# Linear attention and an MoE product: the feature map as a line and a minimum, rest rows on alternate partitions

## Chip, cores and metric

The kernel runs on one core of a Trainium2 chip. The metric is device time in microseconds (us), the median over runs; a run is one execution. The span of a profile is about 2 us shorter than the time of its run.

## The reference

Eight batches, eight heads, 576 rows of 64 numbers; attention with a feature map in place of the softmax, then two dense products with a gelu between them.

```python
def phi(x):
    return np.where(x > 0, x, np.exp(x) - 1.0) + 1.0
q_p, k_p = phi(q), phi(k)
kv = np.einsum('bhsd,bhse->bhde', k_p, v)
z = np.sum(k_p, axis=2)
num = np.einsum('bhsd,bhde->bhse', q_p, kv)
den = np.einsum('bhsd,bhd->bhs', q_p, z)[..., None] + 1e-06
x = (num / den)            # to [4608 tokens, 512]
h = x @ w_in               # 512 x 2048
g = 0.5 * h * (1.0 + np.tanh(c * (h + 0.044715 * h * h * h)))
out = g @ w_out            # 2048 x 512
```

576 rows are 4 x 128 (the main rows of a tile) and 64 more, the rest rows. A tile of rest rows holds the 64 of one even and one odd batch, 128 partitions in all.

## The kernel before

The schedule is written by hand: each engine runs its instructions in the order of the program. The parts that the argument touches are the first loads and the startup of batch 0.

```python
def load_rest_half(src, t, m, s, eng):
    eng.dma_start(
        out=t[REST * s : REST * (s + 1)],          # REST = 64: batch s of the pair
        in_=src[2 * m + s, :, MAIN:S, :].rearrange("h p d -> p h d"))
# ...
load_rest_half(k, ld["kr", 0], 0, 0, nc.sync)      # first half of k_r: batch 0
load_rest_half(v, ld["vr", 0], 0, 0, nc.sync)
ld["v", 0] = load_main(v, 0, "v_x", nc.sync, parts=2)
w_st = [load_w_in(0), load_w_in(1, None, slice(0, 256))]
ld["k", 1] = load_main(k, 1, "k_x", nc.sync)
load_rest_half(k, ld["kr", 0], 0, 1, nc.sync)      # second half of k_r: batch 1
load_w_in(1, w_st[1], slice(256, 512))
# ...
def phi_into(xp, x, e, hs):
    nc.vector.tensor_scalar(e[:, hs], e[:, hs], 1.0, None, op0=ALU.min)
    # ... for each chunk c:
        nc.vector.scalar_tensor_tensor(
            xp[:, c, hs, :], xv[:, c, hs, :], 0.0, ev[:, c, hs, :], op0=ALU.max, op1=ALU.add)
# ... startup of batch 0 ...
for n, e in (("k", ke), ("q", qe)):
    for s in halves:
        nc.scalar.activation(e[:, s], ld[n, 0][:, s], AF.Exp)
exp_rest_half("kr", kre, 0)                        # partitions 0 to 63 only
keep_warm(36)                                      # 72 small matmuls
# ... phi of k and q ...
for i in range(2):
    transpose_q(i, nc.scalar.copy)
keep_warm(5)
phi_rest_half("kr", kre, 0)
cast_v(0, nc.scalar.copy, halves[0])
cast_vr(0, (0,))
for i in range(2, NP):
    transpose_q(i, nc.scalar.copy)
# ... four kv groups, nab (the attention of one chunk), transposes, then the dense products
```

The names in the profile: `kr_e` is the exp of the rest rows of k, `kr_p` their phi, `t_ps` transposes, `qt` the transposed phi of q, `kv_ps` the groups of phi(k)^T v, `n_ps` a nab, `h_ps` and `o_ps` the two dense products, `w_ps` matmuls without use for the result, the warm-up, that are to keep the clock up.

Of the kernel before, what the change touches and what calls it, by code (L numbers as in the profile page):

```python
# [8 lines left out]
FP32 = mybir.dt.float32  # L9
BF16 = mybir.dt.bfloat16  # L10
# [5 lines left out]
def kernel(  # L16
# [8 lines left out]
):  # L25



    nc = tc.nc
# [45 lines left out]
    def load_rest_half(src, t, m, s, eng):  # L75
        eng.dma_start(
            out=t[REST * s : REST * (s + 1)],
            in_=src[2 * m + s, :, MAIN:S, :].rearrange("h p d -> p h d"),
        )
# [34 lines left out]
    for n in ("kr", "vr", "qr"):  # L114
        ld[n, 0] = prest.tile([P, H, D], FP32, name=n[0] + "_r")
    load_rest_half(k, ld["kr", 0], 0, 0, nc.sync)
# [11 lines left out]
    make_identity(nc, ident)  # L128
    vps = [const.tile([P, H, C, E], BF16, name=f"vp{i}") for i in range(2)]
# [5 lines left out]
    for i in range(2):  # L135
        nc.gpsimd.memset(vps[i][:, :, :, D:E], 1.0)
        for s in range(2):
            nc.gpsimd.memset(vrs[i][s], 0.0)
            nc.gpsimd.memset(vrs[i][s][REST * s : REST * (s + 1), :, D:E], 1.0)
        nc.gpsimd.memset(kvbds[i], 0.0)  # L140
# [22 lines left out]

    def exp_main(name, b):
        e = pe.tile([P, H, C * D], BF16, name=name + "_e")
        nc.scalar.activation(e, ld[name, b], AF.Exp)  # L166
        return e

    def phi_into(xp, x, e, hs):

        nc.vector.tensor_scalar(e[:, hs], e[:, hs], 1.0, None, op0=ALU.min)  # L171
        xv = x.rearrange("p h (c d) -> p c h d", d=D)
        ev = e.rearrange("p h (c d) -> p c h d", d=D)
        for c in range(xp.shape[1]):
            nc.vector.scalar_tensor_tensor(  # L175
                xp[:, c, hs, :], xv[:, c, hs, :], 0.0, ev[:, c, hs, :],
                op0=ALU.max, op1=ALU.add,
            )

    def phi_of(x, e, name):  # L180
        xp = pphi.tile([P, x.shape[2] // D, H, D], BF16, name=name)
        phi_into(xp, x, e, slice(0, H))
        return xp

    def phi_rest(name, m):
        x = ld[name, m]
        e = pe.tile([P, H, D], BF16, name=f"{name}_e{m % 2 if name == 'qr' else ''}")
        nc.scalar.activation(e, x, AF.Exp)
        return lambda: phi.__setitem__((name, m), phi_of(x, e, name + "_p"))

    def exp_rest_half(name, e, s):
        r = slice(REST * s, REST * (s + 1))
        nc.scalar.activation(e[r], ld[name, 0][r], AF.Exp)

    def phi_rest_half(name, e, s):
        r = slice(REST * s, REST * (s + 1))
        nc.vector.tensor_scalar(e[r], e[r], 1.0, None, op0=ALU.min)
        nc.vector.scalar_tensor_tensor(
            phi[name, 0][r, 0], ld[name, 0][r], 0.0, e[r], op0=ALU.max, op1=ALU.add
        )  # L200
# [7 lines left out]
    def cast_vr(m, halves=(0, 1)):  # L208
        for s in halves:
            r = slice(REST * s, REST * (s + 1))  # L210
            nc.vector.tensor_copy(out=vrs[m % 2][s][r, :, 0:D], in_=ld["vr", m][r])
# [103 lines left out]
    ke = pe.tile([P, H, C * D], BF16, name="k_e")  # L315
    qe = pe.tile([P, H, C * D], BF16, name="q_e")
    kre = pe.tile([P, H, D], BF16, name="kr_e")
# [4 lines left out]
    nc.gpsimd.memset(phi["kr", 0][REST:P], 0.0)  # L322
# [16 lines left out]
    for n, e in (("k", ke), ("q", qe)):  # L339
        for s in halves:  # L340
            nc.scalar.activation(e[:, s], ld[n, 0][:, s], AF.Exp)  # L341
    exp_rest_half("kr", kre, 0)
    keep_warm(36)
    for n, xp, e in (("k", kp, ke), ("q", qp, qe)):
        for s in halves:
            phi_into(xp, ld[n, 0], e, s)
# [3 lines left out]
    phi_rest_half("kr", kre, 0)  # L350
    cast_v(0, nc.scalar.copy, halves[0])
    cast_vr(0, (0,))
    for i in range(2, NP):
        transpose_q(i, nc.scalar.copy)
    keep_warm(2)
    for h in range(2):
        if h == 1:
            cast_v(0, nc.vector.tensor_copy, slice(4, 6))
            cast_v(0, nc.scalar.copy, slice(6, 8))
        kv_ps = ps_a.tile([P, 2, 512], FP32, name="kv_ps", tag="a")  # L360
        for i in range(2):
            kv_mm(0, 2 * h + i, kv_ps, i)
        kv_evac(0, kv_ps[:, 0:1], h, nc.scalar.copy)
# [32 lines left out]
    kre1 = pe.tile([P, H, D], BF16, name="kr_e")  # L396
    exp_rest_half("kr", kre1, 1)
# [14 lines left out]
    phi_rest_half("kr", kre1, 1)  # L412
# [109 lines left out]
    def plan_second():  # L522
# [4 lines left out]
        def exps():  # L527
            box["q"] = pe.tile([P, H, C * D], BF16, name="q_e")
            for s in halves:
                nc.scalar.activation(box["q"][:, s], ld["q", b][:, s], AF.Exp)  # L530
            gelu_table()

        def phis():
            phi["q", b] = pphi.tile([P, C, H, D], BF16, name="q_p")
            for s in halves:
                phi_into(phi["q", b], ld["q", b], box["q"], s)
# [166 lines left out]
    def second_half(j):  # L703
# [38 lines left out]
        3, (2, 1, 7), (2, 1, 15), None, (1, 2, 0), (1, 2, 1), None, (2, 1, 12)  # L742
    )
    plan_attention(3, 1, 2, (5, 6, 7, 8), (12, 13, 14, 15))
# [49 lines left out]
```

## Time and profile before

| | before |
|---|---|
| time | 296.47 us (296.12 to 297.66, 3 runs) |
| span of the profile | 293.8 us |
| TensorE busy | 286.3 us, 97% |
| first dense product starts | 20.67 us |
| from there to the end | 273.1 us |
| first exp of k_r | 11.11 us |
| load queue (q1) busy | 50.1% of the span, 147 us |

The lines that bear the bound are in the prediction. Two more are from TensorE's timeline (start, duration, engine and line, operation, output and inputs, count, and in brackets the idle time before and what ended it).

```profile
13.90 0.40 PE L219 MATMUL kv_ps<-vp,k_p 128*128 128x130 bf16 x4
...
15.72 0.40 PE L219 MATMUL kv_ps<-vp,k_p 128*128 128x130 bf16 x4 [0.78 <-DVE vp L203]
```

### The profile page before, as it was taken

To read this page: it belongs to the slowest core of one execution; us is meant where nothing else is said; L and a number is where in the kernel's file an instruction comes from. 1 tells how busy PE (TensorE), PEld (TensorE's weight loads), DVE (VectorE), ACT (ScalarE), POOL (GpSimd) and SP (SyncE) were. 2 spreads that over 40 equal slices of the span, in tenths; PEclk is the share of its full clock that TensorE was granted, GB/s the bytes per second of all DMA engines. 3 is DMA by queue (packets, MB, busy share of 16 engines).
4 is the path that set the end of the run, shared out by engine and by line. 5 is a ranking of instruction groups with operands and counts; after the bars stand their busy time and mean duration, and the time that the engine had idled before them with its cause. 6 is when DMAs were issued, how large, how long until landed. Compare 5 with 4: busy or idle time off the path is not lost.

```text
span 293.8 us, 4318 instructions
## 1 busy us (share of the span) xinstructions
PE 286.3 (97%) x1698; PEld 149.0 (51%) x1698; DVE 132.1 (45%) x244; ACT 159.6 (54%) x222; POOL 37.1 (13%) x56
## 2 busy tenths in 40 slices
PE   8979999999999999999999999999999999999995
PEld 6755456644565544544454445444554444444443
DVE  2969495328689488336524592346241000000002
ACT  4759843579955763567355925682560076017400
POOL 8047548300002500000000000000000000000000
PEclk9999999999999999999999999999999999999999
DMA  7999999991499999629925797304241110021032
GB/s 241 361 382 405 394 386 368 322 383 53 102 332 268 186 279 321 178 58 281 306 73 74 242 296 144 68 6 125 89 56 36 71 71 2 0 95 47 2 71 73
DMA packets 64260, 53.24 MB, mean 181 GB/s; under 512 B 31728, under 2 KB 57584, under 8 KB 64240
## 3 DMA queue, kind: packets, MB, share of 16 engines
q1 hardware_dynamic: 60816, 41.82, 50.1%
q10 hardware_dynamic: 2464, 8.52, 7.5%
q0 software_dynamic: 960, 2.62, 3.8%
q8 instruction: 13, 0.21, 0.3%
q14 instruction: 7, 0.06, 0.0%
HBM read 36.70 MB, written 9.44 MB: 157 GB/s over the span
## 4 chain that ended last, share of the span: by engine, by line
PE 91%; DVE 3%; DMA 3%; ACT 1%; issue 1%; SPq 0%; DVEq 0%
PE h_ps L301 42%; PE o_ps L718 41%; PE n_ps L253 3%; DMA q_x<-in_q_dram 3%; PE kv_ps L219 2%; PE o_ps L687 1%; PE t_ps L276 1%; DVE kvbd L242 1%; DVE x L265 1%; PE kv_ps L226 1%; SPq L67 0%; DVE q_p L175 0%; ACT q_e L341 0%; PE t_ps L247 0%; DVE xt L383 0%
## 5 line engine op out<-in xcount | busy, mean ns | idle before, releaser
L718 PE MATMUL o_ps<-w_out_sb,g 128*128 128x512 bf16 x560 | 124.6, 379 | 0.0
L301 PE MATMUL h_ps<-xt,w_in_sb 128*128 128x512 bf16 (+1 forms) x548 | 119.5, 365 | 0.2
L675 ACT ACTIVATE g<-h_ps 128x512 bf16<-128x512 f32 x144 | 83.8, 598 | 48.1 <-PE h_ps L301 47.6
L718 PEld LDWEIGHTS <-g 128*128 128x128 bf16 x560 | 54.2, 98 | 62.6
L301 PEld LDWEIGHTS <-w_in_sb 128*128 128x128 bf16 x612 | 57.7, 98 | 54.7 <-issue 0.5
L733 ACT COPY o_sb<-o_ps 128x512 f32<-128x512 f32 x18 | 10.6, 586 | 56.5 <-PE o_ps L718 56.5
L731 DVE COPY o_sb<-o_ps 128x512 f32<-128x512 f32 x17 | 11.7, 688 | 62.4 <-PE o_ps L718 62.3
L265 DVE TENSOR_TENSOR x<-n_ps,r 128x512 bf16<-128x512 f32 x36 | 24.9, 691 | 1.2
L175 DVE SCALAR_TENSOR_TENSOR q_p<-q_x,q_e 128x512 bf16<-128x512 f32 (+1 forms) x40 | 24.1, 663 | 0.3
L175 DVE SCALAR_TENSOR_TENSOR k_p<-k_x,k_e 128x512 bf16<-128x512 f32 (+1 forms) x36 | 22.0, 674 | 0.3
L242 DVE CAST kvbd<-kv_ps 64x260 bf16<-64x260 f32 (+1 forms) x16 | 6.5, 409 | 28.0 <-PE kv_ps L226 27.9
L171 DVE TENSOR_SCALAR k_e<-k_e 128x2048 bf16<-128x2048 bf16 (+1 forms) x9 | 6.3, 705 | 27.6 <-ACT k_e L166 22.9
L263 DVE RECIPROCAL r<-n_ps 128x8 f32<-128x8 f32 x36 | 7.4, 206 | 24.6 <-PE n_ps L253 24.6
L301 PE MATMUL h_ps<-xt_rest,w_in_sb 128*128 128x512 bf16 x64 | 14.0, 379 | 0.0
L328 PE MATMUL w_ps<-warm 128*128 128x252 bf16 x94 | 12.7, 295 | 1.1 <-DVE warm L127 1.1
L253 PEld LDWEIGHTS <-qt 128*128 128x128 bf16 x128 | 9.7, 98 | 7.9 <-issue 1.1
L166 ACT ACTIVATE k_e<-k_x 128x2048 bf16<-128x2048 f32 x7 | 13.4, 1910 | 0.1
L253 PE MATMUL n_ps<-kvbd,qt 128*128 128x130 bf16 x128 | 12.7, 221 | 0.6 <-ACT kvbd L242 0.3
L219 PEld LDWEIGHTS <-k_p 128*128 128x128 bf16 x128 | 9.7, 96 | 6.8 <-issue 1.4
L219 PE MATMUL kv_ps<-vp,k_p 128*128 128x130 bf16 x128 | 12.2, 220 | 0.9 <-DVE vp L203 0.8
L145 ACT ACT_TABLE_LOAD x8 | 10.3, 1283 | 4.6 <-DVE o_sb L731 4.5
L166 ACT ACTIVATE q_e<-q_x 128x2048 bf16<-128x2048 f32 x6 | 11.4, 1894 | 0.0
(58 smaller groups left out, 144.6 us busy)
## 6 DMA issues: line engine op xcount, KB each, us to landing
out_dram<-o_sb ACTq DMA_DIRECT2D x16, 512.0 KB, 3.9
k_x<-in_k_dram SPq DMA_DIRECT2D x7, 1024.0 KB, 6.4
v_x<-in_v_dram SPq DMA_DIRECT2D x7, 1024.0 KB, 11.8
q_x<-in_q_dram SPq DMA_DIRECT2D x6, 1024.0 KB, 8.4
w_st<-in_moe_w_out_dram SPq DMA_DIRECT2D x4, 1024.0 KB, 10.8
w_st<-in_moe_w_in_dram SPq DMA_DIRECT2D x3, 1024.0 KB, 8.2
q_x<-in_q_dram SPq DMA_DIRECT2D x4, 512.0 KB, 9.3
k_x<-in_k_dram SPq DMA_DIRECT2D x2, 512.0 KB, 4.2
```

What stands on the lines that cost most here:

```text
L145: nc.scalar.preload_act_table_set("gelu_apprx_tanh_and_others")
L166: nc.scalar.activation(e, ld[name, b], AF.Exp)
L175: nc.vector.scalar_tensor_tensor(xp[:, c, hs, :], xv[:, c, hs, :], 0.0, ev[:, c, hs, :], op0=ALU.max, op1=ALU.add,)
L219: nc.tensor.matmul(dst, lhsT=kp[:, c, P * i : P * (i + 1)], rhs=vps[b % 2][:, 2 * i : 2 * i + 2, c, :], start=(c == 0), stop=False,)
L253: nc.tensor.matmul(n_ps[rows, i // 2, 2 * E * (i % 2) : 2 * E * (i % 2) + 2 * E], lhsT=qt_c[:, i, rows], rhs=kvbd[:, i, :], skip_group_che ...
L265: nc.vector.tensor_tensor(x, n_v[:, :, :, 0:D], r[:, :, :, None].to_broadcast([P, 2, 4, D]), op=ALU.mult,)
L301: nc.tensor.matmul(h_ps[:, tok], lhsT=w_in_sb[:, c, P * m : P * (m + 1)], rhs=xt[:, c, tok], start=(c == 0), stop=(c == KM - 1), skip_grou ...
L328: nc.tensor.matmul(w_ps[:, 0:252], lhsT=warm[:, 0:P], rhs=warm)
L675: nc.scalar.activation(gs[j][:, i, :], ps, AF.Gelu_apprx_tanh)
L718: nc.tensor.matmul(o_pss[t], lhsT=g[:, m, P * t : P * (t + 1)], rhs=w_out_sb[:, m, :], start=(m == 0), stop=(m == MM - 1),)
L731: nc.vector.tensor_copy(dst, o_ps)
L733: nc.scalar.copy(dst, o_ps)
```

## The change

Its intent is to relieve VectorE and to shorten the startup. Phi becomes min(exp(x), max(x + 1, 1)), a line and a minimum on a whole tile in place of one minimum and four fused adds. The rest rows of k and v go to even and odd partitions, so that each half load spreads over all of SBUF's partitions, with a mask that blanks the other batch's rows of v. The first tile of v is cast half by VectorE and half by ScalarE (before, three quarters by ScalarE), one copy of qt moves to VectorE, and batch 3 makes phi of q before phi of k. Cut to its core:

```diff
     def load_rest_half(src, t, m, s, eng):
+        rows = slice(REST * s, REST * (s + 1)) if src is q else slice(s, P, 2)
-            out=t[REST * s : REST * (s + 1)],
+            out=t[rows], in_=...
...
     for n in ("kr", "vr", "qr"):
         ld[n, 0] = prest.tile([P, H, D], FP32, name=n[0] + "_r")
+        if n != "qr":
+            nc.vector.memset(ld[n, 0], 0.0)
...
+    mask = const.tile([P, 2], FP32, name="mask")
+    nc.vector.tensor_reduce(mask, ident.rearrange("p (r s) -> p s r", s=2), axis=..., op=ALU.add)
...
+        nc.vector.tensor_scalar(xp..., by_chunk(x[:, hs]), 1.0, 1.0, op0=ALU.add, op1=ALU.max)
+        nc.vector.tensor_tensor(xp..., xp..., e..., op=ALU.min)
...
-    exp_rest_half("kr", kre, 0)
+    exp_into(kre, ld["kr", 0])
...
-    cast_v(0, nc.scalar.copy, halves[0])
+    phi_line(phi["kr", 0], ld["kr", 0])
+    phi_min(phi["kr", 0], kre)
...
     for h in range(2):
-        if h == 1:
-            cast_v(0, nc.vector.tensor_copy, slice(4, 6))
-            cast_v(0, nc.scalar.copy, slice(6, 8))
+        cast_v(0, nc.vector.tensor_copy, slice(4 * h, 4 * h + 2))
+        cast_v(0, nc.scalar.copy, slice(4 * h + 2, 4 * h + 4))
...
-        3, (2, 1, 7), (2, 1, 15), None, (1, 2, 0), (1, 2, 1), None, (2, 1, 12)
+        3, (2, 1, 7), (1, 2, 0), None, (1, 2, 1), (2, 1, 15), None, (2, 1, 12)
```

More of the change, by code (lines that the diff above doesn't have):

```diff
@@ L75, in load_rest_half @@
     def load_rest_half(src, t, m, s, eng):
+        rows = slice(REST * s, REST * (s + 1)) if src is q else slice(s, P, 2)
         eng.dma_start(
-            out=t[REST * s : REST * (s + 1)],
-            in_=src[2 * m + s, :, MAIN:S, :].rearrange("h p d -> p h d"),
+            out=t[rows], in_=src[2 * m + s, :, MAIN:S, :].rearrange("h p d -> p h d")
         )
@@ L128 @@
     make_identity(nc, ident)
+    mask = const.tile([P, 2], FP32, name="mask")
+    nc.vector.tensor_reduce(
+        mask, ident.rearrange("p (r s) -> p s r", s=2), axis=mybir.AxisListType.X, op=ALU.add
+    )
     vps = [const.tile([P, H, C, E], BF16, name=f"vp{i}") for i in range(2)]
@@ L137 @@
         for s in range(2):
-            nc.gpsimd.memset(vrs[i][s], 0.0)
-            nc.gpsimd.memset(vrs[i][s][REST * s : REST * (s + 1), :, D:E], 1.0)
+            nc.vector.tensor_copy(
+                out=vrs[i][s][:, :, D:E],
+                in_=mask[:, s : s + 1, None].to_broadcast([P, H, 1]),
+            )
         nc.gpsimd.memset(kvbds[i], 0.0)
@@ L162, with by_chunk, exp_into, phi_line @@
     phi = {}
+    def by_chunk(x):
+        return x.rearrange("p h (c d) -> p h c d", d=D)
+    def exp_into(e, x, hs=slice(0, H)):
+        nc.scalar.activation(
+            e[:, :, hs, :].rearrange("p c h d -> p h c d"), by_chunk(x[:, hs]), AF.Exp
+        )
     def exp_main(name, b):
-        e = pe.tile([P, H, C * D], BF16, name=name + "_e")
-        nc.scalar.activation(e, ld[name, b], AF.Exp)
-        return e
-    def phi_into(xp, x, e, hs):
-        nc.vector.tensor_scalar(e[:, hs], e[:, hs], 1.0, None, op0=ALU.min)
-        xv = x.rearrange("p h (c d) -> p c h d", d=D)
-        ev = e.rearrange("p h (c d) -> p c h d", d=D)
-        for c in range(xp.shape[1]):
-            nc.vector.scalar_tensor_tensor(
-                xp[:, c, hs, :], xv[:, c, hs, :], 0.0, ev[:, c, hs, :],
-                op0=ALU.max, op1=ALU.add,
-            )
+        e = pe.tile([P, C, H, D], BF16, name=name + "_e")
+        exp_into(e, ld[name, b])
+        return e
+    def phi_line(xp, x, hs=slice(0, H)):
+        nc.vector.tensor_scalar(
+            xp[:, :, hs, :].rearrange("p c h d -> p h c d"), by_chunk(x[:, hs]),
+            1.0, 1.0, op0=ALU.add, op1=ALU.max,
+        )
+    def phi_min(xp, e, hs=slice(0, H)):
+        nc.vector.tensor_tensor(
+            xp[:, :, hs, :], xp[:, :, hs, :], e[:, :, hs, :], op=ALU.min
+        )
     def phi_of(x, e, name):
         xp = pphi.tile([P, x.shape[2] // D, H, D], BF16, name=name)
-        phi_into(xp, x, e, slice(0, H))
+        phi_line(xp, x)
+        phi_min(xp, e)
         return xp
@@ L186, in phi_rest @@
         x = ld[name, m]
-        e = pe.tile([P, H, D], BF16, name=f"{name}_e{m % 2 if name == 'qr' else ''}")
-        nc.scalar.activation(e, x, AF.Exp)
+        e = pe.tile([P, 1, H, D], BF16, name=f"{name}_e{m % 2 if name == 'qr' else ''}")
+        exp_into(e, x)
         return lambda: phi.__setitem__((name, m), phi_of(x, e, name + "_p"))
-    def exp_rest_half(name, e, s):
-        r = slice(REST * s, REST * (s + 1))
-        nc.scalar.activation(e[r], ld[name, 0][r], AF.Exp)
-    def phi_rest_half(name, e, s):
-        r = slice(REST * s, REST * (s + 1))
-        nc.vector.tensor_scalar(e[r], e[r], 1.0, None, op0=ALU.min)
-        nc.vector.scalar_tensor_tensor(
-            phi[name, 0][r, 0], ld[name, 0][r], 0.0, e[r], op0=ALU.max, op1=ALU.add
-        )
     def cast_v(b, fn, s=slice(0, H)):
@@ L209, in cast_vr @@
         for s in halves:
-            r = slice(REST * s, REST * (s + 1))
-            nc.vector.tensor_copy(out=vrs[m % 2][s][r, :, 0:D], in_=ld["vr", m][r])
+            nc.vector.tensor_scalar(
+                vrs[m % 2][s][:, :, 0:D], ld["vr", m], mask[:, s : s + 1], None, op0=ALU.mult
+            )
     def kv_mm(b, i, kv_ps, at_i=None):
@@ L313, in first_mm_early @@
         first_mm(j, m, hs[j, m], slice(0, MAIN // 2))
-    ke = pe.tile([P, H, C * D], BF16, name="k_e")
-    qe = pe.tile([P, H, C * D], BF16, name="q_e")
-    kre = pe.tile([P, H, D], BF16, name="kr_e")
+    ke = pe.tile([P, C, H, D], BF16, name="k_e")
+    qe = pe.tile([P, C, H, D], BF16, name="q_e")
+    kre = pe.tile([P, 1, H, D], BF16, name="kr_e")
     kp = pphi.tile([P, C, H, D], BF16, name="k_p")
@@ L321 @@
     phi["kr", 0] = pphi.tile([P, 1, H, D], BF16, name="kr_p")
-    nc.gpsimd.memset(phi["kr", 0][REST:P], 0.0)
     qt = pt.tile([P, C, NP, P], BF16, name="qt")
@@ L340 @@
         for s in halves:
-            nc.scalar.activation(e[:, s], ld[n, 0][:, s], AF.Exp)
-    exp_rest_half("kr", kre, 0)
+            exp_into(e, ld[n, 0], s)
+    exp_into(kre, ld["kr", 0])
     keep_warm(36)
@@ L345 @@
         for s in halves:
-            phi_into(xp, ld[n, 0], e, s)
+            phi_line(xp, ld[n, 0], s)
+            phi_min(xp, e, s)
     for i in range(2):
@@ L349 @@
     keep_warm(5)
-    phi_rest_half("kr", kre, 0)
-    cast_v(0, nc.scalar.copy, halves[0])
+    phi_line(phi["kr", 0], ld["kr", 0])
+    phi_min(phi["kr", 0], kre)
     cast_vr(0, (0,))
     for i in range(2, NP):
-        transpose_q(i, nc.scalar.copy)
+        transpose_q(i, nc.scalar.copy if i == 2 else nc.vector.tensor_copy)
     keep_warm(2)
     for h in range(2):
-        if h == 1:
-            cast_v(0, nc.vector.tensor_copy, slice(4, 6))
-            cast_v(0, nc.scalar.copy, slice(6, 8))
+        cast_v(0, nc.vector.tensor_copy, slice(4 * h, 4 * h + 2))
+        cast_v(0, nc.scalar.copy, slice(4 * h + 2, 4 * h + 4))
+    for h in range(2):
         kv_ps = ps_a.tile([P, 2, 512], FP32, name="kv_ps", tag="a")
@@ L395 @@
     ke1 = exp_main("k", 1)
-    kre1 = pe.tile([P, H, D], BF16, name="kr_e")
-    exp_rest_half("kr", kre1, 1)
+    kre1 = pe.tile([P, 1, H, D], BF16, name="kr_e")
+    exp_into(kre1, ld["kr", 0])
     gelu_table()
@@ L411 @@
     phi["k", 1] = phi_of(ld["k", 1], ke1, "k_p")
-    phi_rest_half("kr", kre1, 1)
+    phi_line(phi["kr", 0], ld["kr", 0])
+    phi_min(phi["kr", 0], kre1)
     wo_st = [load_w_out(0)]
@@ L527, in exps @@
         def exps():
-            box["q"] = pe.tile([P, H, C * D], BF16, name="q_e")
+            box["q"] = pe.tile([P, C, H, D], BF16, name="q_e")
             for s in halves:
-                nc.scalar.activation(box["q"][:, s], ld["q", b][:, s], AF.Exp)
+                exp_into(box["q"], ld["q", b], s)
             gelu_table()
@@ L535, in phis @@
             for s in halves:
-                phi_into(phi["q", b], ld["q", b], box["q"], s)
+                phi_line(phi["q", b], ld["q", b], s)
+                phi_min(phi["q", b], box["q"], s)
         def cast_vs():
@@ L741 @@
     plan_prepare(
-        3, (2, 1, 7), (2, 1, 15), None, (1, 2, 0), (1, 2, 1), None, (2, 1, 12)
+        3, (2, 1, 7), (1, 2, 0), None, (1, 2, 1), (2, 1, 15), None, (2, 1, 12)
     )
-    plan_attention(3, 1, 2, (5, 6, 7, 8), (12, 13, 14, 15))
+    plan_attention(3, 1, 2, (7, 8, 9, 10), (12, 13, 14, 15))
     for b in range(4, B):
```

## The prediction

> **What bounds the kernel now.** I read the engine shares and the chain that ended last first, then the timeline of the first 24 us one engine at a time, then the DMA view of single stretches for landings.
>
> ```profile
> PE 286.3 (97%) x1698; PEld 149.0 (51%) x1698; DVE 132.1 (45%) x244; ACT 159.6 (54%) x222; POOL 37.1 (13%) x56
> ...
> PE 91%; DVE 3%; DMA 3%; ACT 1%; issue 1%; SPq 0%; DVEq 0%
> ```
>
> The reader is to see that TensorE bounds the whole, and that the 45% of VectorE, which most of the change relieves, hardly stands on the chain. From the first product at 20.67 us on, 512-column matmuls follow each other at 0.216 us and the gaps that I find (evacuations of kvbd near 47 and 77 us, the last xt copy near 54 and 85 us) sum to about 1.1 us of 273. So only the first 20.67 us can move the end by much. There:
>
> ```profile
> 10.14 1.06 ACT L341 ACTIVATE q_e<-q_x 128x1024 bf16<-128x1024 f32 x1 [0.95 <-DMA q_x<-in_q_dram]
> 11.11 0.61 ACT L193 ACTIVATE kr_e<-k_r 64x512 bf16<-64x512 f32 x1
> 11.63 1.04 ACT L337 COPY qt<-t_ps 128x512 bf16<-128x512 bf16 x2
> 12.57 1.05 ACT L203 CAST vp<-v_x 128x1024 bf16<-128x1024 f32 x1
> 13.52 1.06 ACT L337 COPY qt<-t_ps 128x512 bf16<-128x512 bf16 x2
> ...
> 20.65 1.91 ACT L166 ACTIVATE k_e<-k_x 128x2048 bf16<-128x2048 f32 x1
> 22.59 0.63 ACT L193 ACTIVATE kr_e<-k_r 64x512 bf16<-64x512 f32 x1
> ```
>
> ScalarE is a queue in order: the exp of the first rest rows (partitions 0 to 63) stands ahead of all copies of qt. The rest rows of the second batch have an exp of their own, 11 us later. TensorE in the same time:
>
> ```profile
> 10.42 1.22 PE L336 MATMUL t_ps<-ident,q_p 128*128 128x128 bf16 x8
> 11.48 1.24 PE L328 MATMUL w_ps<-warm 128*128 128x252 bf16 x10
> 12.55 1.08 PE L336 MATMUL t_ps<-ident,q_p 128*128 128x128 bf16 x8
> ...
> 17.45 0.51 PE L253 MATMUL n_ps<-kvbd,qt 128*128 128x130 bf16 x6 [0.34 <-ACT kvbd L242]
> ...
> 20.67 1.04 PE L301 MATMUL h_ps<-xt,w_in_sb 128*128 128x256 bf16 x8
> ```
>
> And when the two late loads land, from the DMA view of the stretch 11 to 12 us (last column: us from issue to landing):
>
> ```profile
> k_x<-in_k_dram SPq DMA_DIRECT2D x1, 1024.0 KB, 10.2
> k_r<-in_k_dram SPq DMA_DIRECT2D x1, 128.0 KB, 9.7
> ```
>
> This k_r is the second half of the rest rows, issued at 11.40 us: it lands at 11.40 + 9.7 = 21.1 us. The DMA engines are full here (the page has a 9 in every slice from 7 to 66 us), so it can't come much sooner.
>
> **What the Trainium skill says.** (1) "VectorE: DVE Perf Modes", the perf-mode tier table: 2048 fp32 elements through a one-source op from SBUF take 1227 ns, a two-source op 1224 ns in bf16 and 2293 ns with fp32. The trace agrees where it can: the cast of v (f32 to bf16, 2048 elements) took 1222 ns, four two-source ops on 512 f32 each 2.50 us. (2) The same page, "Zero memsets can be issued as uint32": a memset costs a cycle per element. The trace: 126 elements in 163 ns, so I estimate 512 at 0.56 us. (3) "TensorE: Matmul & The Clock Gate", Part 1: after an idle window of some 3.4 us the array runs at half rate until it has been busy for about as long. The trace shows the start of that: warm-up matmuls average 418 ns around 3 us and 271 ns from 5 us on. (4) "SBUF — State Buffer", Door 1: partitions 0 to 63 reach 8 of 16 DMA ports; every second partition reaches all. No trace here tests it yet; it would help 128 KB loads by tenths of a us.
>
> **The change part by part.**
>
> Feature map: a full tile before is one min (0.69 us) and four adds (2.50), 3.2 us; after, a line x+1, max 1 (1.22, as the cast of v) and a min in bf16 (1.22), 2.45 us. Over 13 full-size tiles that is about 10 us of VectorE work, nearly all beside a busy TensorE: worth nothing there. For q's second half at the start: it lands at 10.12, its exp ends at 11.21 as before, the line (half of 1.22 and a fixed part, 0.69) lies beside the exp, only the min (0.69) follows: q_p at 11.9 instead of 13.13 us, 1.2 us sooner.
>
> Memsets: two of 512 f32 now stand on VectorE before the one that the warm-up waits for: 2 x 0.56 = 1.1 us. The 72 warm-up matmuls, 1.05 to 10.42 us, end at 11.5, so the transposes start 1.1 us later. With the fixed pads behind them, the second pair of transposes starts at 11.5 + 0.44 + 1.07 = 13.0 us, against 12.55. Most of the 1.2 us is given back.
>
> v by both engines: one of the copies of qt moves to VectorE, and all casts of v now stand before the first evacuation, so the waits for v ahead of the third and fourth kv groups (0.78 and 0.16 us) go. Laid out from the row lengths (0.52 a copy, 0.62 a cast on ScalarE, 0.41 on VectorE), this would bring the last nab start from 17.45 to about 16.7 us: 0.8 us saved, if nothing else happened.
>
> The new wait: something else happens. Before, the exp covered partitions 0 to 63, which the first rest load alone fills. Now the rows of the two batches are interleaved, so the exp and the line take all 128 partitions, and both k_r loads are written ahead of that exp in the program. In the order of built instructions this exp waits for the first load's semaphore and for the second's: a count of 32 on the semaphore that q's second half (16) and then the second k_r load raise. The VectorE line waits for the same 32; and the second exp of k_r, at 22.59 us before, has lost its DMA wait. v_r is free of it, as its second load stands later in the program. So ScalarE stops at 11.2 and goes on at 21.1 us.
>
> From there: exp to 21.75, copies of qt to 22.3, 22.8, 23.3; the fourth transpose needs the PSUM buffer that the first copy frees, so TensorE stands idle from 13.3 to 22.35 us, far over the idle window: I take it at half rate at first. Transposes and their copy on VectorE to 23.4; v casts on VectorE to 24.0 and 24.5 (GpSimd's weight casts beside them stretch them; a similar op took 1.33 instead of 0.69 us at 22.59), on ScalarE to 23.95 and 24.6. Four kv groups at half rate (5 matmuls of 0.11, 0.54 each) from 24.05 to 26.2, drained 26.4; evacuations 0.29 and 0.27 with their gaps to 27.05. The last nab start is then 27.1 against 17.45: +9.6 us. The way to the first product was 3.2 us; the slower array adds an estimated 0.4. Sum: +10.0 us at the first product.
>
> Behind it TensorE's work is the same instruction for instruction, so the shift stays. Loads and weight casts, which don't wait for this, get about 10 us of slack.
>
> Batch 3's q first: kv moves from slot 5 to slot 7. VectorE has line, min, line, min, v cast, 5 x 1.22 = 6.1 us from 84.9, to 91.0 in the old clock; slot 7 begins at 89.38 + 8 x 0.216 = 91.1. No gain, and at most 0.2 us lost.
>
> Sum: 296.5 + 10.0 = 306.4 us, rounded.
>
> **The rivals.** (a) The wait costs nothing, because the second load comes early: then +0.8 us is won and the time is about 295.7. Against it: 21.1 us by the landing, and the second load sits behind 1 MB of k in a full queue. Rows spread over all ports would save tenths. (b) The startup gets shorter but weights or q of batch 1 become the bound: phi of batch 1's q ended at 41.54 with its transposes at 41.65, no margin, so the old feature map would have eaten such a gain; the new one frees it. Only matters with (a). (c) The array stays warm through the stop: then the last nab start comes 1.1 us sooner, the 0.4 falls away, and the shift is about 8.5, 305.0 us. (d) It stays at half rate into the dense products: the first 3.4 us of these would lose 1.7 us, about 308. For (c) speaks that no profile here shows an idle of 9 us; for (d), that TensorE is only partly busy from 22 to 30 us. I take the middle.
>
> **Range and chances.** From (c) with a landing half a us sooner, 304.4, to (d), 308.4. Faster than 290.5 isn't within reach of a 20 us startup that loses no work: 0.01. Within 2% needs a shift under 5.9 us, which only (a) gives: 0.05. Slower: 0.94.
>
> **What would show it.** ScalarE's k_r exp, 128 partitions, starts at about 21 us after some 10 us idle ended by DMA k_r. The first warm-up matmul starts at 2.1 to 2.2 us. The line and the min on 2048 elements read near 1.22 us each. The first product starts at 30 to 31 us, matmuls near 23 to 26 us at twice their length; from there to the end some 273 us as before. I am wrong if the k_r exp starts near 11 us; if the DMA view has the second k_r landing well before 20; or if time is lost or won after the first product.

## More of the kernel before

```profile
GB/s 241 361 382 405 394 386 368 322 383 53 102 332 268 186 279 321 178 58 281 306 73 74 242 296 144 68 6 125 89 56 36 71 71 2 0 95 47 2 71 73
...
q1 hardware_dynamic: 60816, 41.82, 50.1%
```

A group of four kv matmuls takes 0.40 us at full clock. One slice is 7.3 us; up to the ninth slice, some 66 us, the loads run without a pause.

## The result, and the profile after

The changed kernel took 307.33 us (306.95 to 307.6, 4 runs) where the kernel before took 297.07 (4 runs): slower, ratio 1.0332, 95% interval 1.0267 to 1.0397. A ratio here is the mean time of one kernel's fast runs over that of the other's fast runs of the same rounds, so it is not quite the ratio of the medians.

From the page after: busy time of the engines, then the chain that ended last by engine, then the clock that TensorE was granted, in tenths, by slice.

```profile
PE 286.4 (94%) x1669; PEld 150.9 (49%) x1698; DVE 114.9 (38%) x196; ACT 158.9 (52%) x221; POOL 32.6 (11%) x47
...
PEclk9955999999999999999999999999999999999999
...
PE 89%; DMA 3%; DVE 3%; SPq 3%; issue 1%; ACT 0%; DVEq 0%; ACTq 0%
```

VectorE has lost 17 us of work (132.1 to 114.9), as the change intended, and TensorE has as much as before, but the span is 11.3 us longer. The clock fell to half in the third and fourth slice, 15 to 30 us. The timelines of ScalarE and of VectorE after, each around the stop:

```profile
10.56 1.06 ACT L177 ACTIVATE q_e<-q_x 128x1024 bf16<-128x1024 f32 x1 [0.51 <-DMA q_x<-in_q_dram]
22.57 0.63 ACT L177 ACTIVATE kr_e<-k_r 128x512 bf16<-128x512 f32 x1 [10.95 <-DMA k_r<-in_k_dram]
23.11 1.54 ACT L345 COPY qt<-t_ps 128x512 bf16<-128x512 bf16 x3
```

```profile
11.65 0.69 DVE L194 TENSOR_TENSOR q_p<-q_p,q_e 128x1024 bf16<-128x1024 bf16 x1 [0.28 <-ACT q_e L177]
22.52 0.43 DVE L188 TENSOR_SCALAR kr_p<-k_r 128x512 bf16<-128x512 f32 x1 [10.18 <-DMA k_r<-in_k_dram]
```

The exp of k_r was on 64 partitions and started at 11.11 us; it is now on 128 and starts at 22.57, after 10.95 us of waiting for a DMA. ScalarE and VectorE wait for the same transfer. TensorE's timeline after shows what that does to it:

```profile
2.14 9.90 PE L336 MATMUL w_ps<-warm 128*128 128x252 bf16 x72 [2.14 <-DVE warm L130]
...
13.39 0.61 PE L344 MATMUL t_ps<-ident,q_p 128*128 128x128 bf16 x8
23.73 1.00 PE L336 MATMUL w_ps<-warm 128*128 128x252 bf16 x4 [9.73 <-ACT qt L345]
25.41 0.61 PE L228 MATMUL kv_ps<-vp,k_p 128*128 128x130 bf16 x4 [0.69 <-DVE vp L211]
...
31.88 1.04 PE L310 MATMUL h_ps<-xt,w_in_sb 128*128 128x256 bf16 x8
```

TensorE named ScalarE's copy of qt as the releaser, but that copy was itself behind the exp: one follows a wait through the engines until it ends at something that had to come from outside, here the second half load of k_r. The DMA view of the stretch 11 to 12.5 us (last column: us from issue to landing) gives its landing; it was issued at 11.97 us.

```profile
k_r<-in_k_dram SPq DMA_DIRECT2D x1, 128.0 KB, 10.5
```

11.97 + 10.5 = 22.47 us, a tenth before the exp starts. The first dense product came at 31.88 us against 20.67, 11.2 us later; from there to the end are 305.1 - 31.88 = 273.2 us, as before (273.1). All of the loss lies before the first product. The windows view (stretch, its length, busy time of PE, PEld, DVE, ACT and POOL with counts, then granted clock, DMA share, GB/s) shows when the clock fell and came back:

```profile
14.00:16.00 2.00, 0.00 (x0) 0.00 (x0) 0.00 (x0) 0.00 (x0) 0.00 (x0) 1.00 1.06 373
16.00:20.00 4.00, 0.00 (x0) 0.00 (x0) 0.00 (x0) 0.00 (x0) 2.56 (x3) 0.56 1.10 341
...
28.00:30.00 2.00, 1.97 (x15) 1.45 (x14) 1.17 (x5) 0.26 (x1) 1.31 (x2) 0.50 1.04 382
30.00:32.00 2.00, 1.66 (x25) 1.36 (x24) 1.89 (x5) 1.48 (x3) 1.49 (x2) 0.97 1.08 357
```

Work stopped at 14.00 us. A mean of 0.56 in four us that begin at 1.0 and go on at 0.5 puts the drop near 16.5 us; a mean of 0.97 puts the return near 30.1. The kv groups in between took 0.61 in place of 0.40 us.

### The profile page after: what moved, and what is told of

It is laid out like the page before. It is cut to its first block, busy times and chain, and to the rows that moved or that the text cites. A ratio compares the mean times of both kernels' runs of the same rounds, so it can differ in the third digit from the quotient of the medians.

```text
span 305.1 us, 4221 instructions
## 1 busy us (share of the span) xinstructions
PE 286.4 (94%) x1669; PEld 150.9 (49%) x1698; DVE 114.9 (38%) x196; ACT 158.9 (52%) x221; POOL 32.6 (11%) x47
## 3 DMA queue, kind: packets, MB, share of 16 engines
q1 hardware_dynamic: 60816, 41.82, 51.9%
## 4 chain that ended last, share of the span: by engine, by line
PE 89%; DMA 3%; DVE 3%; SPq 3%; issue 1%; ACT 0%; DVEq 0%; ACTq 0%
PE h_ps L310 40%; PE o_ps L729 39%; DMA k_r<-in_k_dram 3%; PE n_ps L262 3%; PE kv_ps L228 3%; SPq L68 2%; PE o_ps L698 1%; PE t_ps L285 1%; PE kv_ps L235 1%; SPq L91 1%; DVE kvbd L251 1%; SPq L78 0%; DVE vr L145 0%; PE w_ps L336 0%; DVE vp L211 0%
## 5 line engine op out<-in xcount | busy, mean ns | idle before, releaser
L729 PEld LDWEIGHTS <-g 128*128 128x128 bf16 x560 | 54.2, 98 | 62.6
L744 ACT COPY o_sb<-o_ps 128x512 f32<-128x512 f32 x18 | 10.5, 585 | 60.5 <-PE o_ps L729 60.5
L336 PE MATMUL w_ps<-warm 128*128 128x252 bf16 x94 | 14.2, 316 | 11.9 <-ACT qt L345 9.7
L194 DVE TENSOR_TENSOR k_p<-k_p,k_e 128x2048 bf16<-128x2048 bf16 (+1 forms) x9 | 10.0, 1107 | 22.2 <-ACT k_e L177 22.1
L336 PEld LDWEIGHTS <-warm 128*128 128x128 bf16 x94 | 10.4, 113 | 13.9 <-issue 9.8
L177 ACT ACTIVATE k_e<-k_x 128x2048 bf16<-128x2048 f32 (+1 forms) x9 | 15.5, 1721 | 3.0 <-DMA k_x<-in_k_dram 3.0
L177 ACT ACTIVATE q_e<-q_x 128x2048 bf16<-128x2048 f32 (+1 forms) x10 | 15.5, 1558 | 2.4 <-DMA q_x<-in_q_dram 2.4
L228 PEld LDWEIGHTS <-k_p 128*128 128x128 bf16 x128 | 10.3, 102 | 6.6 <-DVE vp L211 1.2
L194 DVE TENSOR_TENSOR q_p<-q_p,q_e 128x2048 bf16<-128x2048 bf16 (+1 forms) x10 | 10.1, 1012 | 9.0 <-ACT q_e L177 8.3
L154 ACT ACT_TABLE_LOAD x8 | 10.3, 1283 | 1.7 <-DVE vp L211 0.8
```

What stands on the lines that cost most here:

```text
L154: nc.scalar.preload_act_table_set("gelu_apprx_tanh_and_others")
L177: nc.scalar.activation(e[:, :, hs, :].rearrange("p c h d -> p h c d"), by_chunk(x[:, hs]), AF.Exp)
L194: nc.vector.tensor_tensor(xp[:, :, hs, :], xp[:, :, hs, :], e[:, :, hs, :], op=ALU.min)
L228: nc.tensor.matmul(dst, lhsT=kp[:, c, P * i : P * (i + 1)], rhs=vps[b % 2][:, 2 * i : 2 * i + 2, c, :], start=(c == 0), stop=False,)
L336: nc.tensor.matmul(w_ps[:, 0:252], lhsT=warm[:, 0:P], rhs=warm)
L729: nc.tensor.matmul(o_pss[t], lhsT=g[:, m, P * t : P * (t + 1)], rhs=w_out_sb[:, m, :], start=(m == 0), stop=(m == MM - 1),)
```

## The experiments

Theory A: the time is the wait of the 128-partition exp for the second half load, and nothing else of the change costs much. Rival B: other parts (two more memsets on VectorE, the order of the casts, the masked rows) cost a part of it. Rival C: the stop matters mostly through the clock that falls. When the first runs confirmed A, a second question came up: with the wait gone, why was nothing gained? The runs went on three chips; each is compared with the runs of the kernel before (297.39, 297.88 and 297.91 us, 11 runs each).

### The second half load moved below its first reader

```diff
-    load_rest_half(k, ld["kr", 0], 0, 1, nc.sync)        # among the first loads
-    load_w_in(1, w_st[1], slice(256, 512))
...
     phi_min(phi["kr", 0], kre)
+    load_rest_half(k, ld["kr", 0], 0, 1, nc.sync)
+    load_w_in(1, w_st[1], slice(256, 512))
```

The same transfers in the same queue and order; only the program now reads k_r before it writes the other half. It is zero there by the change's own memset.

> The changed kernel with the second k_r load (and the half of w_in behind it) moved below the first exp, line and min of k_r in the program, so that these wait for the first load alone; the order of the loads in the queue is kept. Wait theory: the whole loss goes, the k_r exp starts near 11.7 us, the first product near 20 us, and the time is 296.0 us, 0.0 to 0.8 us under the kernel before. Rival, loads: every second partition makes the start-up loads land later (the second k_r landed 1.4 us later than before, q's second half 0.4), and that costs several us by itself: then 299 or more remains. Rival, VectorE: the added memsets and mask work in front of the warm-up cost the time: then also over 298.

Measured: 297.16 us (6 runs), ratio 0.9992 [0.9965, 1.0019]. The 10 us are gone. ScalarE's timeline, and then TensorE's:

```profile
10.93 0.61 ACT L175 ACTIVATE kr_e<-k_r 128x512 bf16<-128x512 f32 x1
```

```profile
19.68 1.04 PE L308 MATMUL h_ps<-xt,w_in_sb 128*128 128x256 bf16 x8
...
26.39 8.81 PE L308 MATMUL h_ps<-xt,w_in_sb 128*128 128x512 bf16 x40 [1.10 <-POOL w_in_sb L156]
...
39.14 3.61 PE L729 MATMUL o_ps<-w_out_sb,g 128*128 128x512 bf16 x16 [0.49 <-POOL w_out_sb L163]
```

The exp of 128 partitions starts with no wait, which shows A: neither the interleaving nor the wider exp costs the 10 us, only the place of a load in the program. The first product came 1.0 us sooner than in the profile before (19.68 against 20.67), but TensorE then stood 1.6 us for weights that GpSimd casts, where the kernel before stands for none. The cast that ended the 1.10 us, in the profile before and here:

```profile
22.34 1.04 POOL L149 CAST w_in_sb<-w_st 128x1024 bf16<-128x1024 f32 x1 [2.96 <-DMA w_st<-in_moe_w_in_dram]
```

```profile
24.24 2.09 POOL L156 CAST w_in_sb<-w_st 128x1024 bf16<-128x1024 f32 x1 [3.60 <-DMA w_st<-in_moe_w_in_dram]
```

It began when its transfer landed, 1.9 us later than before, and it also took 1.05 us longer, beside VectorE's minimum for batch 1's k (24.20 to 25.42 us). Both had to come together for this wait: a cast of 1.04 us from 24.24 would have ended at 25.28, as the wait began (26.39 - 1.10 = 25.29).

### The kernel before, with its first exp of k_r on all partitions

```diff
-    exp_rest_half("kr", kre, 0)
+    nc.scalar.activation(kre, ld["kr", 0], AF.Exp)
```

> The kernel before with one edit: its first exp of k_r takes all 128 partitions instead of 64, and so waits for both loads; feature map, rows, casts and order are the old ones. Wait theory: this alone loses 9 to 11 us, 306 to 308 us, with the k_r exp starting when the second k_r lands, at about 21.1 us. If the loss comes from the other parts of the change, this one stays within 1 us of the kernel before.

Measured: 310.16 us (4 runs), ratio 1.0421 [1.0383, 1.0458]. ScalarE's timeline:

```profile
23.16 0.63 ACT L342 ACTIVATE kr_e<-k_r 128x512 bf16<-128x512 f32 x1 [10.93 <-DMA k_r<-in_k_dram]
```

One line of the change, put alone into the kernel before, makes the whole loss and more; the wait is sufficient as well as necessary. The size was missed by over 2 us: the old startup leaves more behind the wait (casts of v after the evacuations, and the clock stayed low until about 34 us; its first product came at 34.01).

### The changed kernel, kept busy through the wait

```diff
-    keep_warm(5)
+    keep_warm(48)
```

> The changed kernel with 86 more warm-up matmuls between the two pairs of transposes, which fill TensorE's idle stretch from 13 to about 22.6 us. If the half clock after the stop is a term of the loss of its own, as the prediction has it (0.54 instead of 0.29 us a kv group, and 0.4 us later), the time falls by 1.0 to 1.5 us, to about 306.0, the granted clock stays at 1.0 and the kv matmuls read their old length. If the half clock is hidden behind ScalarE and VectorE, the time stays within 0.3 us of 307.3.

Measured: 306.7 us (4 runs), ratio 1.0321 [1.0281, 1.0362]. TensorE's timeline:

```profile
13.16 10.48 PE L336 MATMUL w_ps<-warm 128*128 128x252 bf16 x96
...
25.45 0.41 PE L228 MATMUL kv_ps<-vp,k_p 128*128 128x130 bf16 x4 [0.92 <-DVE vp L211]
...
30.67 1.04 PE L310 MATMUL h_ps<-xt,w_in_sb 128*128 128x256 bf16 x8
```

The kv groups are back at 0.41 us and the first product came 1.2 us sooner than in the changed kernel (30.67 against 31.88). Counted from the first kv group, so that the landing of the load plays no part, the way to it is 5.22 us in place of 6.47. So of the 11.2 us the half clock had about 1.2 and the wait the rest; C falls. In the medians the gain is 0.6 us, between the two branches of the expectation, and the intervals of the two ratios overlap: the gain in time is not shown.

### A control, and less to load

The kernel before, unchanged, was run as if it were an experiment, to know how far its own profile moves.

> The kernel before, unchanged, for its trace on the same chip as the runs of this call, since the landings of the first four experiments were later than those of the profile before (first piece of w_in cast at 17.6 us instead of 16.4). If that is the chip, this trace shows the late landings too; if it is the changed loads, it shows 16.4 us again. Its time is that of the kernel before by construction.

Measured: 297.99 us (2 runs) beside 297.88; its first product came at 21.63 us, a microsecond later than in the first profile of the same kernel. So a difference of 1 us in the startup between single profiles on different chips means little.

For the question of the weights, the late-load kernel was run with half of batch 1's k left out (zeroed by GpSimd; wrong, though phi of zero is near that of these small inputs and the comparison passed).

```diff
-    ld["k", 1] = load_main(k, 1, "k_x", nc.sync)
+    ld["k", 1] = pld.tile([P, H, C * D], FP32, name="k_x", tag="ld")
+    # load heads 0 to 3 only; memset heads 4 to 7 on gpsimd
```

> The first experiment's kernel with a wrong result on purpose: half of batch 1's k is not loaded but set to zero, 0.5 MB less ahead of w_in's last pieces and of w_out. If the 1.0 us that the first experiment gains up to the first product is lost again to weights that land too late (TensorE's waits for w_in of 1.1 and 0.3 us and for w_out of 0.5), these waits shrink to nearly nothing and the time is 1.0 to 1.8 us under the first experiment's, 295.5 to 296.2. If they only cover other waits, it stays within 0.4 us of it.

Measured: 295.98 us (6 runs), ratio 0.9941 [0.9925, 0.9958], and no wait for weights left. With 512 KB less ahead of them, the weights are there in time. Against the control the first product is 1.2 us sooner (20.40 against 21.63), and from there to the end it takes 273.1 us as before, where the late load took 275.1. So it was the wait for the weights that ate what the startup had gained.

The same kernel with the two memsets moved from VectorE to GpSimd, to let the warm-up start sooner:

```diff
-            nc.vector.memset(ld[n, 0], 0.0)
+            nc.gpsimd.memset(ld[n, 0], 0.0)
```

> The first experiment's kernel with the two memsets of k_r and v_r moved from VectorE to GpSimd, so that the warm-up matmuls start at 1.05 instead of 2.14 us. The first product comes 0.6 to 0.9 us sooner than in the first experiment (about 18.9 us). If the weights' landing is what bounds the stage behind it, the time stays within 0.3 us of the first experiment's and TensorE's wait for w_in grows by that much; if not, it falls by the 0.6 to 0.9 us.

Measured: 297.08 us (6 runs), ratio 0.9997 [0.9970, 1.0023]. TensorE's timeline of the late load, and then of this kernel:

```profile
2.14 9.50 PE L334 MATMUL w_ps<-warm 128*128 128x252 bf16 x72 [2.14 <-DVE warm L128]
```

```profile
1.06 10.84 PE L334 MATMUL w_ps<-warm 128*128 128x252 bf16 x72 [1.06 <-DVE warm L128]
```

The warm-up started at 1.06 us instead of 2.14, and in this profile nothing came of it: its 72 matmuls took 10.84 us in place of 9.50, so the first transposes, whose half of q's phi had been ready at 9.88 us, began at 11.73 (11.47 in the late load). The first product was at 19.94 us, not near 18.9 as expected, and TensorE still waited 0.9 us for weights. The same 72 matmuls take 9.30 to 10.84 us in the profiles (419 ns each while slow, 271 later, though the granted clock in the profile reads 1.00 throughout); among the three with the startup of the kernel before it is 9.33 to 10.65. So part of what moves the first product from profile to profile is the length of the warm-up, not the edit.

### Rest rows back in halves

The late-load kernel with the rows of k and v on partitions 0 to 63 and 64 to 127, as before the change. This was to tell what the alternate rows are worth.

```diff
-        rows = slice(REST * s, REST * (s + 1)) if src is q else slice(s, P, 2)
+        rows = slice(REST * s, REST * (s + 1))
...
-        mask, ident.rearrange("p (r s) -> p s r", s=2), ...
+        mask, ident.rearrange("p (s r) -> p s r", s=2), ...
```

> The first experiment's kernel with the rest rows of k and v back on partitions 0 to 63 and 64 to 127 and the mask made to fit; everything else the same. If the spread over every second partition is what made the early loads land later, q's second half lands at 10.1 instead of 10.5 us here and the time is 0.2 to 0.5 us under the first experiment. If the spread helps, [...]it is some tenths over it. If the landings vary by themselves, the two are equal within 0.2 us.

Measured: 303.12 us (6 runs, one of them slow), ratio 1.0204 [1.0157, 1.0251], 6 us worse than with alternate rows: all three branches of the expectation were wrong. It was repeated on the second chip.

> The fourth experiment's kernel once more, ahead of the others of its kind this time, because it ran last and scattered (300.9 to 305.5 us). If consecutive halves of the partitions cost that much in the new kernel, it is 3 us or more over the kernel before again; if the chip had grown slower, it is within 1 us of it.

Measured: 303.32 us (6 runs, one of them slow), ratio 1.0152 [1.0104, 1.0200]. So it is no accident of one chip. TensorE's timeline of the repeat names where the time goes:

```profile
28.49 8.96 PE L308 MATMUL h_ps<-xt,w_in_sb 128*128 128x512 bf16 x40 [1.58 <-POOL w_in_sb L156]
...
42.56 3.61 PE L729 MATMUL o_ps<-w_out_sb,g 128*128 128x512 bf16 x16 [1.66 <-POOL w_out_sb L163]
```

With 0.92 us for a cast of v and 2.37 for transfers of q_p into qt, that makes 6.5 us of waits for loads or for work behind loads. But the kernel before has its rows in halves too and pays nothing of the kind. Something else in the changed kernel had to take part, and the page shows a trace of it in every kernel with the change: the load queue moved the same 41.82 MB, but more slowly. From the page of the late-load kernel with alternate rows:

```profile
GB/s 222 343 343 384 370 358 354 295 327 289 112 346 270 188 240 307 180 73 252 322 86 72 215 335 130 56 18 125 89 56 36 71 71 2 0 88 54 2 71 71
...
q1 hardware_dynamic: 60816, 41.82, 53.3%
```

Slices 2 to 6 run at 343 to 384 GB/s, where the kernel before has 361 to 405, and the queue is busy 0.533 x 294.8 = 157 us against 147. With the rows in halves it was 54.2% of 302.2, 164 us.

### One tile of 8 bytes

The addresses in the built programs gave a suspect. The change adds a mask of two numbers for each partition, 8 bytes, which take 32. It lies ahead of the tiles that the loads fill, and shifts all of them: the first k tile begins at byte 71168 with the mask grown to 256 bytes, a multiple of 256 (in the kernel before the load tiles begin at such multiples too), and at byte 70944 with the small mask, 32 bytes past one. "DMA: Bandwidth & Descriptors" of the Trainium skill, section "How a descriptor splits into AXI transactions", says that a read which does not begin at a multiple of 256 bytes starts its first transaction at the multiple below, and that the bytes fetched for nothing still cost beats. It describes this for reads and gives no figure for a write; here the loads write to the tiles, so the page suggests the experiment and does not settle it.

```diff
-    mask = const.tile([P, 2], FP32, name="mask")
+    mask_t = const.tile([P, 64], FP32, name="mask")
+    mask = mask_t[:, 0:2]
```

Four kernels were run with this edit. The late load alone:

> The first late-load kernel with one tile grown: the mask takes 256 bytes of a partition in place of 8, so that every tile that a load fills begins at a multiple of 256 bytes again, as in the kernel before (71168 for the first k tile; 70944 in the changed kernel, which is 32 bytes past such a multiple). Theory of the alignment: the loads go as fast as before, the load queue is busy about 50% of the span (53 to 54% in the kernels with the 8-byte mask), the second weight cast starts near 23.2 us in place of 24.2, the product waits under 0.4 us for weights in place of 1.6, and the time falls to 0.3 to 1.5 us under the kernel before. Rival, that the alternate rows or another order of the transfers slow them: 297.2 us again, queue 53 to 54%, the same waits.

Measured: 295.66 us (6 runs), ratio 0.9927 [0.9898, 0.9957]. Its page:

```profile
GB/s 241 372 383 400 394 393 384 358 357 29 140 345 259 174 272 291 172 59 288 296 77 73 239 317 127 69 5 137 77 56 36 71 71 2 0 94 49 2 71 72
...
q1 hardware_dynamic: 60816, 41.82, 50.6%
```

Slices 2 to 6 are back at 372 to 400 GB/s, the queue is busy 148 us, GpSimd's cast of the later half of w_in's second piece (the expectation's "second weight cast") started at 22.59 us (24.24 with the small mask), and TensorE waited for no weight. The same work at the same addresses modulo 256 runs as before, and the intervals with the small and the large mask lie apart in all three pairs; the theory of the alignment stands. All four ran on one chip, on which the small mask didn't run; but on the other two chips the queue was busy 147 us (the control) and 149 us (the full exp), both without a mask, and 155 to 164 us with the small mask, so the chip doesn't make the difference. What is not told apart is which multiple it takes: 64 or 128 bytes were not tried. With GpSimd's memset as well:

> The late load with GpSimd's memset and the 256-byte mask, the best kernel that the parts so far give. Theory of the alignment: as the run with VectorE's memset or up to 0.3 us better, 295.2 to 296.5 us where the kernel before takes 297.4, ratio 0.993 to 0.998. Rival: 297.1 us as with the 8-byte mask.

Measured: 295.16 us (294.37 to 295.48, 6 runs), ratio 0.9908 [0.9879, 0.9938], the lowest median, though its interval overlaps that of the run before. Its first product came at 18.40 us. Of the 1.9 us that this is sooner than in the run before (20.28), 1.1 is the earlier start of the warm-up and 0.8 its length (9.30 against 10.10 us), which the edit doesn't set. And 0.9 was lost again behind it (274.1 us to the end in place of 273.2), of which the trace names only 0.2, a wait for weights. With the rows in halves:

> The late load with the rest rows of k and v in halves, as before the change, and the 256-byte mask; with the 8-byte mask this took 303.1 and 303.3 us. If the 32-byte offset is what slowed the loads and the halves are harmless, as they are in the kernel before: 296 to 297.5 us, load queue about 50%. If the halves themselves cost it (without the change's alternate rows each half load fills 64 neighbouring partitions only): still 301 to 303 us. In between: both have a share.

Measured: 297.41 us (6 runs), ratio 0.9978 [0.9944, 1.0013]; load queue 50.3%. The 6 us fall to 1.75 (297.41 against 295.66; the two intervals overlap slightly). So the small loss of the halves and the 32 bytes make each other worse: with alternate rows the 32 bytes cost some 2 us (0.9992 against 0.9927 of 298), with halves some 6 (the mean of 1.0204 and 1.0152 against 0.9978). Why they compound isn't shown. And the old feature map in the late-load kernel:

```diff
-        nc.vector.tensor_scalar(xp..., by_chunk(x[:, hs]), 1.0, 1.0, op0=ALU.add, op1=ALU.max)
-        nc.vector.tensor_tensor(xp..., xp..., e..., op=ALU.min)
+        nc.vector.tensor_scalar(e..., e..., 1.0, None, op0=ALU.min)
+        for c in range(xp.shape[1]):
+            nc.vector.scalar_tensor_tensor(xp[:, c]..., x[:, c]..., 0.0, e[:, c]..., op0=ALU.max, op1=ALU.add)
```

> The late load with the 256-byte mask and the feature map of the kernel before (a minimum with 1 and four fused maximum-and-add instructions a tile, in place of the line, and one minimum). The new map saves VectorE nearly half of its work a tile, but VectorE was busy 50% of the span before and sets no end in this stage: within 0.3 us of the aligned late load. If the new map is worth something on its own: 0.5 to 2 us later, with TensorE waiting for a transposed phi.

Measured: 298.03 us (6 runs), ratio 1.0013 [0.9980, 1.0046], 2.4 us later than with the new map: the expectation's first branch was wrong, and its second named another wait than the one found. (Its 50% for VectorE is 45% on the page of the kernel before.) TensorE's timeline names the place, and VectorE's what stood there:

```profile
92.58 0.40 PE L229 MATMUL kv_ps<-vp,k_p 128*128 128x130 bf16 x4 [1.20 <-DVE vp L212]
```

```profile
85.75 2.50 DVE L194 SCALAR_TENSOR_TENSOR q_p<-q_x,q_e 128x512 bf16<-128x512 f32 x4
...
88.89 2.50 DVE L194 SCALAR_TENSOR_TENSOR k_p<-k_x,k_e 128x512 bf16<-128x512 f32 x4
91.30 1.22 DVE L212 CAST vp<-v_x 128x2048 bf16<-128x2048 f32 x1
```

With the new map the same cast of v began at 89.54 us and nobody waited for it:

```profile
89.54 1.22 DVE L210 CAST vp<-v_x 128x2048 bf16<-128x2048 f32 x1
```

An engine at 45% of the span still has its dense moments. Batch 3's q before its k puts two phis ahead of the cast of v; with the faster map that just fits. So this run charges to the old map an order that the kernel before didn't have: 1.2 of the spans' 1.7 us lie there, 0.4 at the startup (first product 20.64 against 20.28). The old map with the old order wasn't run in this base.

### All runs

| kernel | mask | median us | ratio | interval |
|---|---|---|---|---|
| after | 8 B | 307.33 | 1.0332 | 1.0267 to 1.0397 |
| before, exp on all partitions | none | 310.16 | 1.0421 | 1.0383 to 1.0458 |
| after, kept busy | 8 B | 306.70 | 1.0321 | 1.0281 to 1.0362 |
| late load | 8 B | 297.16 | 0.9992 | 0.9965 to 1.0019 |
| late load, GpSimd's memset | 8 B | 297.08 | 0.9997 | 0.9970 to 1.0023 |
| late load, 512 KB less | 8 B | 295.98 | 0.9941 | 0.9925 to 0.9958 |
| late load, halves | 8 B | 303.12, 303.32 | 1.0204, 1.0152 | 1.0157 to 1.0251, 1.0104 to 1.0200 |
| before, control | none | 297.99 | 1.0009 | 0.9969 to 1.0049 |
| late load | 256 B | 295.66 | 0.9927 | 0.9898 to 0.9957 |
| late load, GpSimd's memset | 256 B | 295.16 | 0.9908 | 0.9879 to 0.9938 |
| late load, halves | 256 B | 297.41 | 0.9978 | 0.9944 to 1.0013 |
| late load, old map | 256 B | 298.03 | 1.0013 | 0.9980 to 1.0046 |

## Why the prediction was right

It held: 306.4 us with 304.4 to 308.4 (its own terms, 296.5 and 10.0, sum to 306.5), and 307.33 was measured, by the mechanism that it named. Point by point:

- **The new wait** was predicted as 21.1 us for the start of the exp, ended by k_r; it was 22.57. The first run shows it necessary and the second sufficient. The landing was 1.4 us off; the load was issued 0.6 us later than before and took 0.8 us longer. Whether the 32 bytes had a part in that is not shown. In the kernel before with the full exp, whose tiles are aligned, the exp started at 23.16, so a late landing needs no 32 bytes; but slices 2 to 6 of the changed kernel run at 341 to 384 GB/s in place of 361 to 405.
- **The halt of TensorE** was predicted because the fourth transpose would lack a PSUM buffer. That was wrong: all four groups of transposes ran before 14.0 us, and it was the warm-up matmuls after them that waited for the copy of qt. The stop was the same but ended later: 23.73 instead of 22.35 us, as the copy was later.
- **The half clock** was predicted with kv groups of 0.54 us a group of five, and they came every 0.54 us (25.41, 25.93, 26.47, 27.01). Rival (c), a warm array, was to be 1.5 us better; keeping the array warm brought 1.2 at the first product, and nothing clear of noise in the time. Rival (d) fell: the clock was back near 30.1 us, ahead of the dense products.
- **The memsets** took 0.48 us each, not 0.56; the warm-up started at 2.14, within the predicted 2.1 to 2.2.
- **Line and minimum** on 2048 elements took about 1.22 us each and half tiles 0.69, as predicted. Phi of q's second half was ready at 12.34 us, not 11.9: q landed later. The saving on VectorE was put at about 10 us and is 17; it stands beside a busy TensorE, so the time doesn't show it.
- **The shift** was predicted as 10.0 us at the first product: 11.2 in the two profiles, with the same 273 us behind it as predicted; in the medians of the same rounds it is 10.3. First product: 31.88, not "30 to 31". The step that was mis-sized is the landing of the second half load, 1.5 us late at the exp; behind it the sum held. From the exp to the last nab start it was 5.9 us (22.57 to 28.43) where the prediction has 6.0, and from there to the product 3.4 where it has 3.6.
- **Rival (a)**, no wait, was given 295.7 us. The run that has no wait took 297.16; the term that (a) lacks is the weights, which land 1 to 2 us later with the change's tile addresses. With these mended it is 295.66; that this is so near to 295.7 is luck, as (a) meant 0.8 us under the kernel before and this is 2.2 under the 297.91. Rival (b) had weights as the next bound, and that is what the 512 KB less showed.
- **"Nearly all beside a busy TensorE: worth nothing there"**, of the feature map, was not the whole of it: with batch 3's q first, the old map makes TensorE wait 1.2 us. The two parts belong together, which the prediction took as two.
- **What the prediction missed altogether** is the 8-byte mask. Its effect on the changed kernel itself was not measured: the changed kernel with a 256-byte mask wasn't run, and behind a 10 us wait the weights have slack.

## What to carry to other kernels

When an instruction is widened to more partitions, ask which loads have written what it now reads, and where these stand in the program: here the load written later than its reader cost nothing, and the same load written earlier cost its whole landing time. Look at the addresses after adding any small tile ahead of load buffers; here 8 bytes slowed the loads whose tiles they shifted. And when a mended wait brings less than its length, follow the next wait with the profile: here the gain reappeared as soon as the weights did.

## What the Trainium skill lacked or had wrong

- "DMA: Bandwidth & Descriptors", "How a descriptor splits into AXI transactions": the cost of an unaligned start is told for reads, in beats, and without a cost in time. Loads from device memory into SBUF tiles that begin 32 bytes past a multiple of 256 kept the queue busy 157 us in place of 148 for the same 41.82 MB, and cost some 2 us of 298, some 6 with the rest rows in halves.
- "SBUF — State Buffer", Door 1, by which partitions 0 to 63 reach only half of the ports, agrees in direction: aligned, rest rows on alternate partitions were 1.75 us faster than in halves (295.66 against 297.41 us). That the loss grows to some 6 us with tiles off by 32 bytes is on no page that was read.
- "TensorE: Matmul & The Clock Gate", Part 1, gives some 3.4 us both to lose and to regain the clock. Here it was lost about 2.5 us after the last matmul (14.0 to near 16.5 us) and regained about 6.4 us after the restart (23.73 to near 30.1), with small matmuls and gaps in between. The page does say that the window runs free.
- "VectorE: DVE Perf Modes", "Zero memsets can be issued as uint32": a cycle per element, whatever the type. Two memsets of 512 f32 took 485 ns each, and 126 elements of uint32 took 163 ns. So an element costs (485 - 163) / 386 = 0.83 ns and the rest, about 0.06 us, is fixed, which the page doesn't give. The prediction's 0.56 us reckons 1.03 ns for each further element and was 16% too high.
